# Cross network on one core: the first layer's weights in three loads, and a searched order begun 24 chunks sooner

## The chip, the cores and the metric

One core of a Trainium2 chip. TensorE multiplies into eight accumulator banks (PSUM); ScalarE (ACT in the profile) and VectorE (DVE) take results out; SyncE (SP) issues nearly all transfers; GpSimd (POOL) does little here. The metric is the device time of one execution in microseconds, the median of several; less is better.

## The reference

A cross network of six layers over 16384 rows of 416 features, in bf16:

```python
x = x0
for l in range(L):                                   # L = 6
    proj = jnp.einsum('bd,de->be', x, ws[l]) + bs[l]  # 416 x 416 weights
    x = x0 * proj + x
return x
```

## The kernel before, in words

**Tiles.** Data lies transposed: features on the 128 partitions, rows along the free axis. 416 features are three tiles of 128 and a tail of 32. The rows form eight groups of 2048, a group has four chunks of 512. A job (g, l) is layer l of group g. For each output tile i and chunk j it needs a product with three input tiles and with the tail: 13 quarters of 32 input rows. The tails of up to three jobs are made together, as a batch (`tails`, L700). ScalarE reads each finished bank and adds the bias (`tw`), VectorE multiplies by x0 and adds x (`x`). For tails the same is done into `ts` and `x3`.

**Recording.** `add` (L35) records each operation with what it reads and writes; `emit` (L149) writes the engines' queues and the semaphore waits out of that. Within an engine the order of recording is the order of execution, but for VectorE's sums, which can be held back by one place.

**The start.** `first_job` (L845) does job (0, 0). Group 0 is loaded in its natural layout by eight transfers (`load_nat`, L762; chunk j, halves of 2). TensorE turns it with an identity (`transposed_chunk`, L809), in two halves of six transposes each, and VectorE and ScalarE copy the results out of the banks (L828, L830). The first products (L673, by `full`) take the columns 0 to 256 of the first layer's weights, which one transfer brings (L772; the other columns come later, L777). `keep_busy` (L794) gives TensorE filler products. Then comes the first job's tail (L708, L720), and group 1.

**The written order.** After `first_job` the items (tiles and batches, in job order) up to the second output tile of job (0, 2) are written out whole tile by whole tile: `two_tiles` (L1141) for the first two tiles of job (1, 0), then the loop at L1160, which lets tail rows of two neighbouring tiles stand next to each other (`mode`). Products are full (L673), by columns of 32 (L667) or by rows of 32 (L694); four of the latter two kinds run beside each other.

**The searched run.** From there to the closing part, `stream` (L1085) splits every product into its 13 row quarters and places them on TensorE's four row strips independently. The order comes from a table: `ORDER` (L204) is a long text in which each letter names a strip and how old the chunk is that it turns to, and `|` stands for a batch of tails. `replay` (L231) walks through the table with fixed costs in units (20 to a product; `READ`, `NEXT`, `BACK` and so on for the reading engines), gives each product its place and each chunk its bank, and starts a chunk no sooner than a bank is free and its inputs from the layer before should be done (`needs`). Row products are L1129 (input tiles) and L1133 (tails); each finished chunk goes to `evacuate_chunk` (L562; L574 on ScalarE, L586 and L594 on VectorE). In a batch inside the run the second job's tail is read by VectorE alone (L636), the others by ScalarE (L640) and VectorE (L642); L644 is the tail sum.

**The end.** The last job of the last group is computed in natural layout (L1194), so that its results need no turning.

**Queues.** SyncE issues, in this order: two row loads, the first weights, six row loads, the tail weights of layer 0 (L401), the remaining columns, group 1's transposing loads (L411, L421), layers 1, 2 and 3, group 2, and so on.

Of the kernel before, what the change touches and what calls it, by code (L numbers as in the profile page):

```python
# [3 lines left out]
P = 128  # L4
CH = 512
# [16 lines left out]
class Program:  # L22
# [179 lines left out]
READ, NEXT, BACK, SECOND, PAIR, TAILS, SUMS = 19, 56, 70, 110, 56, 220, 240  # L202
LETTERS = "ABCDEFGHIJKLMNOPQRSTUVWXYZabcdefghijklmnopqrstuvwxyz0123456789"
ORDER = (  # L204
    "ABCDMBCTZOELBaAjZSIfFiQPVKHYBCcTVIDSJATKBQLWBQXKNALCZQLWBQCbMRLWBITWBQPCZMLWRALSBQLCRIbCRAPeJYWH"
    "N|AWPJQGDQBDWNITCJnQCZTIWBLQWNALWBQXCNIDWZIDWJYTCRbIWBLQBSbINWHAVCTUBOQLBaTARaDQZOLUSBDUORbICJbA"
    "aVTMGBPYBWPIRaHAORDYKBXQKBTIWBDUOZITCZIOTFADeRYPCNIbWQFPK|ABPWAVKPQBCPQVKDAVePQBKfMRaHJAbSIBKTAZ"
    "SLcNHCBQXBSMLBaAOXZQKHMVSDBQOXBMKXAVKDQVKDBMebUJOHAVObIRCLQBSfJ|EODBTAOZACbVcPKFAeXRYGPBYWPRAKPQ"
    "BiLMRGDNACbNAaXNISHBYCTNYCbVISPFAePBUKDVQaDRIOXFAOXBAObVQGLBcCXNAePZIWTFASPBcKPRUGDNAWDNQXCJAbWR"
    "APSJYDaRUDSJUfOF|ITCRIODJAbSJATJCQDOBPcWJDIeVbQOFXAVODUKBXQKBTIBaLQCZTAOQZLWFPAWNDUCNTUBOTIBaLQN"  # L210
    "WALVCQXBOQLBaTINWDIVODUCNXAOJXAWJDUeYBXOIZHSUBTOIBbCMZDWIZTO|EBPWQBOLAVCPQVKfMFSDARWPANXCUNSDIBS"
    "XYBTKAReLMVSbIBKTAhSLYNHCBQXNCMLWBAaPQVKDQBaPBUKjMZSXEBSPAZKPQVHCBQWDMRKXBIWDVAOXJAWfYJTCQZOLEBW"
    "DcRCTMJWbERKP|ABPWQBKPAVCPQVKDANebUBKXQNaHJASXIBKTAhSLYNHCBQXNCMLWBAaXQNKHAZWTMBKDYRKXNAWDNQXBOQ"
    "BObIRWDQBOTICfZAXaRIPFCYPBaUPCMVaLBIWDVQCPRICfJAebJUSPFAaPQVGL|MBDSNAPKBAObRUGLBAeXNYKHVAWTJAKTY"
    "BLCYRWDRIOXBIWPBUOLRAKbBAWPZQCLRYCbNIWTBISPBYKPRAeDQVPKAJXCURCPQJaDIBafQVGPBMaXRIOH|ABTOAZKPQBKD"
    "BUPaAVKbQdCbMRWLEBWTARKPYBWDNQKDZISXBIOTBAOfRYKDZQLWBQKXARKXMBWLBQCPZAWbJQGDQZWPBIWPQBOLAVCPQVKj"
    "MFSDARWPANXCUNSLEBSDYRCTIBafIVOTE|BPWRALOBcDOZQKXBIDVaITCRIbBSYLBSIXNaALVOQDKBQXKBITBaQLVOADOZXA"
    "WJAXSJYDSJYXOFQDZOAXBOQXBOQLBaITVCQDSZMLWBIXSBQLOBIbCZQLCZITWBQLBaITNWALVCUTBSATNaIDJWYTBSPAdOXY"
    "SF|AODVPAKNYXCBQXaJcHORAPaRIHCBUbCRMLWBIWTBQKPVALWRMGDBQCbRMWLBAWbNAKPZUCXQJaPBIWPBcKPVAWLMRCLBQ"
    "XCRMLWFAWTBQCPZAaPJAWbJMSDZcPCNXYSF|AOTBPAaBYSPJUGDdQODJMbWBIXOdAXKNQHCBQWDMRCbJAaTVIODJAfaUBXSc"  # L220
    "NKHAZSXIBLCVYLSNEXCMBWPIBWLAVCXQBOTAdaPUBOLQVaHJAbCMZSLUBSLARKfARWLMBKDYRCPRIbWBQXJOALBaQVCPISXB"
    "ASPYVKHMBCbNQeDJMSXZIP|FCATBaQPBOIDaVIDSJYDSZMXGJTASBjMCNULCVITBeQLNWADaRXMCJDYSBQPaJAbWRAjSJUPG"
    "dQLOBAPSBYPCVIPSBIDSVYDKRAbeJMXGBXMCVIPSBcLORALiNAXOJQDCNUTBOAXBeQPaBYLOVALWdMTGBYfSVMLG|ABWPAVK"
    "PQBCPVQCPJAebVAWLNQaHBYOXBUOLAVKbMRGDBQWDMRKXAJCbQVOLEBaXABOTYVGLMRWDIBSXIBTKAZSLMBKDQZKXARWDQNX"
    "KBISXNADOBcWbBMSXIZGDRYCTZIWPBIWfNQGLB|AWPRAKPBUCPRUKDJAbeJQPWFICXBUPChMLWFAWTBQKPVAWLNQCLBQCbMR"
    "WDJMWDVISPFAObBUCPVQKfNALWBQWLNACbRMLCYJTWARLW|AJTMWDJUCTVICTJWADVaMTBaNIDKVYTOBAfaNQLVGMTCJMSDA"
    "BXa"
# [3 lines left out]
def replay(tails, events, needs, keep):  # L231
# [15 lines left out]
    home, read, out, latest, due = {}, {}, [], [[]] * 4, list(events)  # L247
# [11 lines left out]
    for letter in ORDER:  # L259
        if letter == "|":  # L260
# [4 lines left out]
            on = at + 3 * SLOT * m + PHASE  # L265
            moved = [on + SLOT * k for k in parts]
# [40 lines left out]
def bass_standalone__cross_network_dcn__recsys_kernel(  # L307
# [82 lines left out]
    def load_wm(l, eng, f0=0, f1=D):  # L390
        toks = {0: [("wm", l)], W0: [("wm", l, "rest")]}[f0] if l == 0 else [("wm", l), ("wm", l, "rest")]
        add(eng, lambda h: h.dma_start(
            wm[l][:, :, f0:f1], ws[l, 0:NT * P, f0:f1].rearrange("(t p) f -> p t f", p=P)),
            writes=toks, lane=f"wm{l}_{f0}", batch=0)

    def wm_tok(l, i):
        return ("wm", l) if i < 2 else ("wm", l, "rest")
# [112 lines left out]
    def evacuate(g, l, i, banks, js, step, vector=()):  # L510
# [21 lines left out]
        while a <= js[-1]:  # L532
            if step > 1 and a % 2 == 0 and a + 1 <= js[-1] and banks[a + 1] == banks[a] + 1:
                w = 2
            else:
                w = 1
# [121 lines left out]
    def full(g, l, i, banks, first, chunk_major, after_chunk=None, chunks=range(NJ), ts_=range(NT), columns=False):  # L658
# [4 lines left out]
        for t, j in seq:  # L663
            if columns:
                for c in range(NJ):
# [5 lines left out]
                        reads=[stok(t, j), wm_tok(l, i)], writes=[("ps", banks[j])])  # L671
# [4 lines left out]
                reads=[stok(t, j), wm_tok(l, i)], writes=[("ps", banks[j])])  # L676
# [3 lines left out]
    def rows32(g, l, i, banks, first, small=False, inner=False):  # L680
        src, stok = x3_src(g, l)
        ecols = slice(i * P, (i + 1) * P)
        for j in range(NJ):
            r, q = quad(g, l, j)
            if small:
                for c in range(NJ):
                    o = slice(c * T32, (c + 1) * T32)
                    add("pe", lambda h, q=q, j=j, r=r, c=c, o=o: h.matmul(
                        psum[o, banks[j] * CH:(banks[j] + 1) * CH],
                        w3[l][q, i * P + c * T32:i * P + (c + 1) * T32], src[q, :],  # L690
                        start=first, stop=not first, tile_position=(r * T32, c * T32)),
                        reads=stok + [("w3", l, r)], writes=[("ps", banks[j])])
                continue
            add("pe", lambda h, q=q, j=j, r=r: h.matmul(  # L694
                bank(banks[j]), w3[l][q, ecols], src[q, :], start=first and not inner,
                stop=not first and not inner,
                tile_position=(r * T32, 0)),
                reads=stok + [("w3", l, r)], writes=[("ps", banks[j])])

    def tails(batch, corners_last=False, banks=None):  # L700
# [14 lines left out]
        for (g, l), b in zip(batch, bs_):  # L715
            src, stok = x_src(g, l)
            for t in range(NT):
                for j in range(NJ):
# [5 lines left out]
                        reads=[stok(t, j), wm_tok(l, NT)], writes=[("ps", b)])  # L724
# [47 lines left out]
    load_wm(0, "sp", 0, W0)  # L772
# [4 lines left out]
    load_wm(0, "sp", W0, D)  # L777
# [31 lines left out]
    def transposed_chunk(j):  # L809
# [3 lines left out]
        for k2 in (0, 2):  # L813
            for t in range(NT):
# [6 lines left out]
            if j == 0 and k2 == 0:  # L821
                keep_busy(2, 3)
        for t in range(NT):
# [20 lines left out]

    def first_job():  # L845
# [211 lines left out]
    mode = {}  # L1057
    prev = None
    for n, it in enumerate(items):
        if it[0] == "tails":  # L1060
            prev = None
        elif prev is None:
            mode[n] = "FR"
            prev = n
        else:
            mode[n] = "RF"
            prev = None
    for n in list(mode):
        if mode[n] == "FR" and not (n + 1 in mode and mode[n + 1] == "RF"):
            mode[n] = "F1"  # L1070

# [13 lines left out]
    def stream(run):  # L1085

        chunks, due = [], []
        for it in run:
            if it[0] == "tails":
                due.append(it[1])  # L1090
            elif it[1] not in order[-3:-1]:
                chunks += [(it[1], it[2], j) for j in range(NJ)]
# [8 lines left out]
        needs += [[]] * NJ  # L1101
        plan, read, left = replay([quad(g, l, j)[0] for (g, l), i, j in chunks] + [quad(LAST, L - 1, j)[0] for j in range(NJ)],
                                  [len(b) for b in due], needs, NJ)
        at = list(ring)
# [4 lines left out]
        for _, r, c, b in plan:  # L1109
# [14 lines left out]
            t = seen[c, r] = seen.get((c, r), -1) + 1  # L1124
            src, stok = x_src(g, l)
            s3, tok3 = x3_src(g, l)
            kw = dict(start=count[c] == 1, stop=count[c] == 4 * NT + 1, tile_position=(r * T32, 0))
            if t < NT:
                add("pe", lambda h, l=l, t=t, j=j, b=b, q=q, ecols=ecols, src=src, kw=kw: h.matmul(  # L1129
                    bank(b), wm[l][q, t, ecols], src(t, j, j + 1)[q, :], **kw),  # L1130
                    reads=[stok(t, j), wm_tok(l, i)], writes=[("ps", b)], row=r)
# [4 lines left out]
            if count[c] == 4 * NT + 1:  # L1136
# [4 lines left out]
    def two_tiles(g, l):  # L1141
# [17 lines left out]
    s_lo = items.index(("tile", (0, 2), 1))  # L1159
# [181 lines left out]
```

## Time and profile before

| | |
|---|---|
| median of 3 runs | 464.73 us (464.65 to 465.34) |
| the profiled execution | 464.88 us |
| its span, first to last instruction | 463.1 us |
| mean granted TensorE clock | 0.999 |
| instructions | 17845 |

The profile lists, by engine, how long it was busy; the timeline lists runs of like instructions by start, length, line, shape and count; a bracket behind a line gives the idle time before it and what ended it. Busy TensorE time overlaps within itself, because a product's end is modelled: the distance from start to start says more than a single length.

### The profile page before, as it was taken

To read this page: it belongs to the slowest core of one execution; us is meant where nothing else is said; L and a number is where in the kernel's file an instruction comes from. 1 tells how busy PE (TensorE), PEld (TensorE's weight loads), DVE (VectorE), ACT (ScalarE), POOL (GpSimd) and SP (SyncE) were. 2 spreads that over 40 slices of the span, in tenths; PEclk is the share of its full clock that TensorE was granted. 3 is DMA by queue.
4 is the path that set the end of the run, shared out by engine and by line. 5 is a ranking of instruction groups with operands and counts; after the bars stand their busy time and mean duration, and the time that the engine had idled before them with its cause. 6 is when DMAs were issued, how large, how long until landed. Compare 5 with 4: busy or idle time off the path is not lost.

```text
span 463.1 us, 17845 instructions
## 1 busy us (share of the span) xinstructions
PE 458.4 (99%) x8001; PEld 266.7 (58%) x8001; DVE 403.2 (87%) x697; ACT 381.9 (82%) x609; POOL 7.7 (2%) x16
## 2 busy tenths in 40 slices
PE   9999999999999999999999999999999999999996
PEld 5444656575655656565665556566556565555552
DVE  2897898988889898898989989898988988989997
ACT  4686889887988889798888979888888888888786
POOL 1000000000000000000000000000000000000010
PEclk9999999999999999999999999999999999999999
DMA  8986859000002859089656965590000079172799
GB/s 233 194 168 142 152 125 191 10 23 9 19 4 36 138 184 192 16 129 219 91 90 127 208 98 91 101 234 24 24 4 4 24 139 299 47 124 52 209 161 314
DMA packets 136128, 53.79 MB, mean 116 GB/s; under 512 B 113642, under 2 KB 134644, under 8 KB 136052
## 3 DMA queue, kind: packets, MB, share of 16 engines
q1 hardware_dynamic: 135896, 52.54, 54.3%
q8 instruction: 62, 1.02, 0.9%
q14 instruction: 14, 0.11, 0.1%
q10 hardware_dynamic: 156, 0.11, 0.1%
HBM read 5.97 MB, written 13.63 MB: 42 GB/s over the span
## 4 chain that ended last, share of the span: by engine, by line
PE 96%; DVE 2%; ACT 1%; issue 0%; DVEq 0%
PE ps L1129 74%; PE ps L720 7%; PE ps L1133 6%; PE ps L673 4%; PE ps L667 1%; PE ps L708 1%; DVE x L1255 1%; DVE x L1249 1%; PE ps L800 1%; PE ps L818 1%; ACT tw L574 1%; PE ps L694 1%; DVE tw L586 0%; DVE x L594 0%; DVE x L1217 0%
## 5 line engine op out<-in xcount | busy, mean ns | idle before, releaser
L1129 PE MATMUL ps<-x,wm 32*128 32x512 bf16 x6288 | 372.8, 374 | 0.0
L574 ACT ACTIVATE tw<-ps,bias 128x512 bf16<-128x512 f32 x524 | 326.9, 688 | 48.8 <-PE ps L1129 35.9
L1129 PEld LDWEIGHTS ps<-x,wm 32*128 32x128 bf16 x6288 | 222.3, 92 | 135.1 <-ACT tw L574 6.4
L586 DVE TENSOR_TENSOR tw<-tw,x 128x1024 bf16<-128x1024 bf16 x262 | 176.7, 688 | 41.1 <-ACT tw L574 39.5
L594 DVE TENSOR_TENSOR x<-tw,x 128x1024 bf16<-128x1024 bf16 x262 | 171.2, 688 | 0.3
L1133 PE MATMUL ps<-x,w 32*128 32x512 bf16 x524 | 159.5, 374 | 0.0
L1133 PEld LDWEIGHTS ps<-x,w 32*128 32x128 bf16 x524 | 44.6, 92 | 5.9
L720 PE MATMUL ps<-x,wm 128*32 128x512 bf16 x564 | 33.6, 380 | 0.0
L640 ACT ACTIVATE ts<-ps,bias 128x512 bf16<-128x512 f32 x32 | 20.4, 685 | 13.1 <-PE ps L708 13.1
L538 ACT ACTIVATE tw<-ps,bias 128x1024 bf16<-128x1024 f32 (+1 forms) x24 | 20.7, 938 | 8.2 <-PE ps L694 7.0
L720 PEld LDWEIGHTS ps<-x,wm 128*32 128x32 bf16 x564 | 13.5, 96 | 18.2 <-ACT tw L574 3.7
L673 PE MATMUL ps<-x,wm 128*128 128x512 bf16 x92 | 21.3, 380 | 0.0
L644 DVE TENSOR_TENSOR x<-ts,x 128x512 bf16<-128x512 bf16 x47 | 18.4, 419 | 0.3
L547 DVE TENSOR_TENSOR tw<-tw,x 128x1024 bf16<-128x1024 bf16 (+1 forms) x21 | 13.0, 636 | 2.2 <-ACT tw L538 2.1
L673 PEld LDWEIGHTS ps<-x,wm 128*128 128x128 bf16 x92 | 8.3, 98 | 11.4 <-issue 2.1
L636 DVE SCALAR_TENSOR_TENSOR ts<-ps,bias,x 128x512 bf16<-128x512 f32 x15 | 11.2, 746 | 3.1 <-PE ps L708 3.1
L552 DVE TENSOR_TENSOR x<-tw,x 128x1024 bf16<-128x1024 bf16 (+1 forms) x21 | 12.6, 634 | 0.0
L642 DVE TENSOR_TENSOR ts<-ts,x 128x512 bf16<-128x512 bf16 x32 | 12.4, 417 | 0.0
L956 POOL COPY ost<-ot 128x512 bf16<-128x512 bf16 x5 | 4.6, 922 | 367.3 <-DMA ot<-x 367.3
L1194 PE MATMUL ps<-wm,x 128*128 128x416 bf16 x48 | 9.3, 340 | 0.0
L828 DVE COPY x<-ps 128x512 bf16<-128x512 bf16 x5 | 2.0, 422 | 8.2 <-PE ps L818 8.1
L1243 ACT ACTIVATE x<-ps 128x416 bf16<-128x416 f32 x16 | 7.7, 529 | 1.5 <-PE ps L1194 1.5
(52 smaller groups left out, 74.1 us busy)
## 6 DMA issues: line engine op xcount, KB each, us to landing
out_dram<-ost SPq DMA_DIRECT2D x6, 1664.0 KB, 8.3
x<-x SPq DMA_DIRECT2D x24, 96.0 KB, 2.2
x<-in_x_dram SPq DMA_DIRECT2D x8, 208.0 KB, 4.2
x<-in_x_dram SPq DMA_DIRECT2D x4, 416.0 KB, 8.1
wm<-in_ws_dram SPq DMA_DIRECT2D x5, 312.0 KB, 3.5
x<-x SPq DMA_DIRECT2D x22, 64.0 KB, 2.5
out_dram<-x SPq DMA_DIRECT2D x3, 416.0 KB, 2.6
out_dram<-ost SPq DMA_DIRECT2D x2, 416.0 KB, 2.8
```

Source lines behind the costliest of these rows:

```text
L538: add("act", lambda h, a=a, w=w, b0=b0: h.activation(tw[r][:, a * CH:(a + w) * CH], psum[:, b0 * CH:(b0 + w) * CH], ACT_F.Identity, bias=b ...
L547: add("dve", lambda h, a=a, e=e: h.tensor_tensor(tw[r][:, a * CH:e * CH], tw[r][:, a * CH:e * CH], x0s[s0][:, i * GC + a * CH:i * GC + e * ...
L552: add("dve", lambda h, a=a, e=e: h.tensor_tensor(xs[so][:, i * GC + a * CH:i * GC + e * CH], tw[r][:, a * CH:e * CH], src(i, a, e), ALU.ad ...
L574: add("act", lambda h: h.activation(tw[r][:, j * CH:(j + 1) * CH], bank(b), ACT_F.Identity, bias=bias[:, i, l:l + 1], scale=1.0), reads=[( ...
L586: add("dve", lambda h: h.tensor_tensor(tw[r][:, o], tw[r][:, o], x0s[s0][:, c], ALU.mult), reads=[("tw", r, k) for k in both] + [x0_tok(s0 ...
L594: add("dve", lambda h: h.tensor_tensor(paired(xs[so][:, c], "p (k j q) -> p j k q"), paired(tw[r][:, o], "p (j k q) -> p j k q"), paired(s ...
L640: add("act", lambda h: h.activation(ts[r][:, :], bank(b), ACT_F.Identity, bias=bias[:, 3, l:l + 1], scale=1.0), reads=[("ps", b), "bias"], ...
L644: add("dve", lambda h: h.tensor_tensor(x3s[so][:, :], ts[r][:, :], res, ALU.add), reads=[("ts", r)] + rtok, writes=[("x3", so), ("x3", so, ...
L673: add("pe", lambda h, t=t, j=j: h.matmul(bank(banks[j]), wm[l][:, t, ecols], src(t, j, j + 1), start=(first and t == 0), stop=(not first a ...
L720: add("pe", lambda h, t=t, j=j, src=src, l=l, b=b, ro=ro, qo=qo: h.matmul(psum[qo, b * CH:(b + 1) * CH], wm[l][:, t, NT * P:D], src(t, j, ...
L1129: add("pe", lambda h, l=l, t=t, j=j, b=b, q=q, ecols=ecols, src=src, kw=kw: h.matmul(bank(b), wm[l][q, t, ecols], src(t, j, j + 1)[q, :], ...
L1133: add("pe", lambda h, l=l, b=b, q=q, ecols=ecols, s3=s3, kw=kw: h.matmul(bank(b), w3[l][q, ecols], s3[q, :], **kw), reads=tok3 + [("w3", l ...
```

## The change

Four things are done together.

1. The first layer's first 256 columns come as three transfers of one input tile each, in the order 1, 0, 2, in place of one.
2. In the first layer's first two chunks, the products go by input tile, both output tiles for each, in the order in which the copies come (`by_copy`, `by_input_tile`); the transposes use the same order; the second half of chunk 2's transposes stands behind chunk 1's products; one filler is 2 and not 5 units of 128 columns.
3. `two_tiles` does the whole first tile of job (1, 0) alone and of the second tile only the products of input tile 0 for chunks 0 and 1; its results are read bank by bank. The loop in written order and `mode` are gone: all other items go to `stream`, which so has 24 more chunks. The first two chunks have one input tile less to do there.
4. `ORDER` is a new table. `replay` knows about the begun chunks (`ahead`), and about when a layer's tail is to be expected after its batch (`TURN`, `SHIFT`); the inputs of the first 36 chunks are expected six products later (`LATE`). The starting times of the banks and of ScalarE are new, and jobs (0, 1) and (0, 2) go by halves of two chunks.

```diff
 FENCE, PHASE, CHANGE = 22, 52, 9
-READ, NEXT, BACK, SECOND, PAIR, TAILS, SUMS = 19, 56, 70, 110, 56, 220, 240
+READ, NEXT, BACK, SECOND, PAIR, TAILS, SUMS, SHIFT = 19, 56, 70, 110, 56, 220, 240, 215
+TURN, LATE = (200, 150, 260), 6
...
-    size = [[3 + (r == tails[c]) if c < n - keep else 2 * (r == tails[c]) for r in range(4)] for c in range(n)]
-    free, flight, begun, act = [0] * 4, {}, 0, 156
-    banks = [(0, 0), (0, 1), (0, 2), (0, 3), (84, 4), (84, 5), (178, 6), (178, 7)]
+    size = [[3 - (c < ahead) + (r == tails[c]) if c < n - keep else 2 * (r == tails[c]) for r in range(4)] for c in range(n)]
+    free, flight, begun, act = [0] * 4, {}, 0, 243
+    banks = [(0, 0), (0, 1), (0, 2), (0, 3), (89, 4), (145, 5), (201, 6), (257, 7)]
...
+        if r == tails[c] and after[c][0] >= 0:
+            start = max(start, ons[after[c][0]] + after[c][1] - 3 * SLOT * (c < n - keep))
...
+    def load_wm_tile(t):
+        add("sp", lambda h: h.dma_start(wm[0][:, t, 0:W0], ws[0, t * P:(t + 1) * P, 0:W0]),
+            writes=[("wm", 0, t)], lane=f"wm0_{t}", batch=0)
...
-    load_wm(0, "sp", 0, W0)
+    for t in (1, 0, 2):
+        load_wm_tile(t)
...
+    def by_copy(j):
+        return (0, 2, 1) if j == 1 else (1, 0, 2)
+
+    def by_input_tile(j, *bks):
+        src, stok = x_src(0, 0)
+        for n, t in enumerate(by_copy(j)):
+            for i, b in enumerate(bks):
+                add("pe", lambda h, n=n, t=t, i=i, b=b: h.matmul(
+                    bank(b[j]), wm[0][:, t, i * P:(i + 1) * P], src(t, j, j + 1),
+                    start=n == 0, stop=False), reads=[stok(t, j), ("wm", 0, t)], writes=[("ps", b[j])])
...
-        keep_busy(5, 3)
+        keep_busy(2, 3)
...
-        full(g, l, 0, ba, True, True, chunks=[0])
-        full(g, l, 1, bb, True, True, chunks=[0])
+        by_input_tile(0, ba, bb)
         transposed_chunk(1)
-        transposed_chunk(2)
-        full(g, l, 0, ba, True, True, chunks=[1])
-        full(g, l, 1, bb, True, True, chunks=[1])
+        transposed_chunk(2, (0,))
+        by_input_tile(1, ba, bb)
+        transposed_chunk(2, (2,))
         transposed_chunk(3)
...
-                chunks += [(it[1], it[2], j) for j in range(NJ)]
+                if it[1] not in order[1:4:2]:
+                    chunks += [(it[1], it[2], j) for j in range(NJ)]
+                elif not it[2]:
+                    chunks += [(it[1], i, j) for a in (0, 2) for i in range(NT) for j in (a, a + 1)]
...
-            needs.append([(t, *p) for t, p in enumerate(pairs) if c - max(p) < 30])
+            needs.append([(t - LATE * (c < 3 * 3 * NJ), *p) for t, p in enumerate(pairs) if c - max(p) < 30])
...
-        for i in (0, 1):
-            full(g, l, i, bks[i], True, False, ts_=[0], columns=True)
+        for i, chunks in ((0, range(NJ)), (1, range(2))):
+            full(g, l, i, bks[i], True, False, chunks=chunks, ts_=[0], columns=True)
         full(g, l, 0, bks[0], True, False, ts_=[1, 2], columns=True)
         rows32(g, l, 0, bks[0], False)
-        evacuate(g, l, 0, bks[0], list(range(NJ)), 2)
-        finish_tile(g, l)
-        rows32(g, l, 1, bks[1], False, inner=True)
-        full(g, l, 1, bks[1], False, False, ts_=[1, 2])
-        evacuate(g, l, 1, bks[1], list(range(NJ)), 2)
+        evacuate(g, l, 0, bks[0], list(range(NJ)), 2, single=True)
         finish_tile(g, l)
...
-    s_lo = items.index(("tile", (0, 2), 1))
-    for n, it in enumerate(items[:s_lo]):
...
-    bka, left = stream(items[s_lo:])
+    _, (g, l), i = items[0]
+    start_job(g, l)
+    two_tiles(g, l)
+    bka, left = stream(items[1:])
```

More of the change, by code (lines that the diff above doesn't have):

```diff
@@ L388, in bass_standalone__cross_network_dcn__recsys_kernel, with load_wm, wm_tok @@
     W0 = 2 * P
-    def load_wm(l, eng, f0=0, f1=D):
-        toks = {0: [("wm", l)], W0: [("wm", l, "rest")]}[f0] if l == 0 else [("wm", l), ("wm", l, "rest")]
+    def load_wm(l, eng, f0=0):
+        toks = [("wm", l, "rest")] if f0 else [("wm", l, t) for t in range(NT)]
         add(eng, lambda h: h.dma_start(
[L393 to L397, printed above, removed]
+            wm[l][:, :, f0:D], ws[l, 0:NT * P, f0:D].rearrange("(t p) f -> p t f", p=P)),
+            writes=toks, lane=f"wm{l}", batch=0)
+    def load_wm_tile(t):
+        add("sp", lambda h: h.dma_start(wm[0][:, t, 0:W0], ws[0, t * P:(t + 1) * P, 0:W0]),
+            writes=[("wm", 0, t)], lane=f"wm0_{t}", batch=0)
+    def wm_tok(l, i, t):
+        return ("wm", 0, "rest") if l == 0 and i > 1 else ("wm", l, t)
     def load_w3(l, eng):
@@ L532, in evacuate @@
         while a <= js[-1]:
-            if step > 1 and a % 2 == 0 and a + 1 <= js[-1] and banks[a + 1] == banks[a] + 1:
+            if not single and step > 1 and a % 2 == 0 and a + 1 <= js[-1] and banks[a + 1] == banks[a] + 1:
                 w = 2
@@ L675, in full, with rows32 @@
                 start=(first and t == 0), stop=(not first and t == NT - 1)),
-                reads=[stok(t, j), wm_tok(l, i)], writes=[("ps", banks[j])])
+                reads=[stok(t, j), wm_tok(l, i, t)], writes=[("ps", banks[j])])
             if after_chunk and t == NT - 1:
                 after_chunk(j)
-    def rows32(g, l, i, banks, first, small=False, inner=False):
+    def rows32(g, l, i, banks, first):
         src, stok = x3_src(g, l)
@@ L684, in rows32 @@
             r, q = quad(g, l, j)
[L685 to L693, printed above, removed]
             add("pe", lambda h, q=q, j=j, r=r: h.matmul(
-                bank(banks[j]), w3[l][q, ecols], src[q, :], start=first and not inner,
-                stop=not first and not inner,
+                bank(banks[j]), w3[l][q, ecols], src[q, :], start=first, stop=not first,
                 tile_position=(r * T32, 0)),
@@ L812, in transposed_chunk @@
         place = ((ba, 0), (bb, 0), (ba, CH)) if j == 0 else ((ba, 0), (ba, CH), (bb, 0))
-        for k2 in (0, 2):
-            for t in range(NT):
+        for k2 in halves:
+            for t in by_copy(j):
                 b, o = place[t]
@@ L822, in transposed_chunk @@
                 keep_busy(2, 3)
+        if 2 not in halves:
+            return
         for t in range(NT):
@@ L1123, in stream @@
             q, ecols = slice(r * T32, (r + 1) * T32), slice(i * P, (i + 1) * P)
-            t = seen[c, r] = seen.get((c, r), -1) + 1
+            begun = c < 2
+            t = seen[c, r] = seen.get((c, r), 0 if begun else -1) + 1
             src, stok = x_src(g, l)
             s3, tok3 = x3_src(g, l)
-            kw = dict(start=count[c] == 1, stop=count[c] == 4 * NT + 1, tile_position=(r * T32, 0))
+            whole = 4 * (NT - begun) + 1
+            kw = dict(start=count[c] == 1 and not begun, stop=count[c] == whole, tile_position=(r * T32, 0))
             if t < NT:
@@ L1130, in stream @@
                     bank(b), wm[l][q, t, ecols], src(t, j, j + 1)[q, :], **kw),
-                    reads=[stok(t, j), wm_tok(l, i)], writes=[("ps", b)], row=r)
+                    reads=[stok(t, j), wm_tok(l, i, t)], writes=[("ps", b)], row=r)
             else:
```

108 lines of the change are left out of this document (40 added, 68 removed).

## The prediction

> **What bounds the kernel now.** I read the page's busy table first, then the chain of waits, then TensorE's timeline up to 45 us, then the copies' engines over the same stretch.
>
> ```profile
> span 463.1 us, 17845 instructions
> PE 458.4 (99%) x8001; PEld 266.7 (58%) x8001; DVE 403.2 (87%) x697; ACT 381.9 (82%) x609; POOL 7.7 (2%) x16
> ...
> PE 96%; DVE 2%; ACT 1%; issue 0%; DVEq 0%
> ```
>
> TensorE is busy 99% of the span and holds 96% of the chain that ended last. So only two things can shorten the run: fewer or denser TensorE instructions, or less waiting inside what shows as busy. The timeline (start, length, line, shape, count) shows where it is not dense:
>
> ```profile
> 5.78 1.53 PE L673 MATMUL ps<-x,wm 128*128 128x512 bf16 x6
> 7.14 1.55 PE L818 MATMUL ps<-ident,x 128*128 128x128 bf16 x24
> 8.54 1.46 PE L673 MATMUL ps<-x,wm 128*128 128x512 bf16 x6
> ...
> 12.36 0.40 PE L694 MATMUL ps<-x,w 32*128 32x512 bf16 x4
> ...
> 14.64 2.76 PE L673 MATMUL ps<-x,wm 128*128 128x512 bf16 x12
> ...
> 18.31 3.62 PE L667 MATMUL ps<-x,wm 128*32 128x512 bf16 x64
> 21.87 0.61 PE L694 MATMUL ps<-x,w 32*128 32x512 bf16 x8
> ...
> 40.48 0.83 PE L1129 MATMUL ps<-x,wm 32*128 32x512 bf16 x12
> ```
>
> Twelve full products take 2.76 us, the last 0.38: (2.76 - 0.38) / 11 = 0.216 us from start to start. I call that a slot; four 32-row or 32-column products share one (64 at 18.31 take 16 slots, 3.46 us; the next line starts at 21.87, so the change of shape costs 0.10). The searched run begins at 40.48 and the closing part (L1194) at 447.77.
>
> **The change, part 1: 24 chunks move into the searched run.** Before, TensorE goes from 18.31 to 40.48 = 22.17 us by written order: 112 L667 (28 slots), 24 L694 (6), 56 L673 (56), 16 L688 (1), 24 L720 (6): 97 slots, 20.95 us, and 8 small L708. So 1.22 us is overhead: the joints between kinds, and those 8. After, the instruction order has 56 of the 32-column kind (14 slots), 4 L694 (1), and 304 more row products in the run (7124 against 6820: 76 slots) with one more batch of tails, two jobs (24 products, 6 slots): the same 97 slots, in fewer kinds.
>
> What the run costs per slot, from its own trace: 447.77 - 40.48 = 407.29 us for 6820 / 4 + 44 x 3 = 1837 slots, 396.8 us, and 15 batches of tails. A batch (L720 at 57.96, run resumed at 60.37, 9 slots between) costs 2.41 - 1.94 = 0.47 beyond its slots; 15 make 7.05. What is left, 3.45 us or 0.85%, are its empty places. So the moved stretch costs 14 x 0.216 + 0.10 + 0.22 (L694) + 82 x 0.216 + 0.47 + 0.85% of 18.2 (0.15) = 21.67 us: **0.50 less** than 22.17. The 0.85% is the old order's; the new order is another one over all 552 chunks, and each tenth of a per cent of it is 0.43 us either way. I keep 0.85% and hold that as a bound.
>
> **Part 2: what is late next.** The run now starts at about 21.7 instead of 40.5, while VectorE still works off the first layer. It is nearly without idle time from 14.2 to 32.3; ScalarE alone frees the accumulators, so VectorE's lag reaches TensorE only through next-layer inputs. Those of group 0, layer 1 end at 22.78 (its last L552) and 23.57 (its tail, L644). In the new order the first product that reads that layer comes 4 to 5 slots after the run's start, at 22.7, and reads first the tile that has been done since 17; the tail is read after 25.8. No wait. The first that can bite is the tail of layer 2 of group 0. In the new order its first reader stands 14 products of its row behind the first batch, 14 x 0.216 = 3.03 us after the run resumes. Behind that product stand all four rows, and the accumulators they would free. What the tail takes on VectorE is counted from these rows:
>
> ```profile
> 192.64 0.75 DVE L636 SCALAR_TENSOR_TENSOR ts<-ps,bias,x 128x512 bf16<-128x512 f32 x1 [0.33 <-PE ps L708]
> 193.31 0.68 DVE L594 TENSOR_TENSOR x<-tw,x 128x1024 bf16<-128x1024 bf16 x1
> 193.91 0.69 DVE L586 TENSOR_TENSOR tw<-tw,x 128x1024 bf16<-128x1024 bf16 x1
> 194.51 0.42 DVE L644 TENSOR_TENSOR x<-ts,x 128x512 bf16<-128x512 bf16 x1
> ...
> 31.95 0.75 DVE L644 TENSOR_TENSOR x<-ts,x 128x512 bf16<-128x512 bf16 x2
> ```
>
> The resume there was at 192.49. In the new order VectorE has, from the batch on: one L636 (0.67 to the next start), a product of 1024 (0.60), a tail sum (0.34), a sum of 1024 (0.60), a tail product (0.34), the tail sum (0.42). Begun 0.15 after the resume, it ends at 3.12, and TensorE starts 0.06 later: 3.18 against 3.03, a **wait of 0.15**. The bounds: the first job's tail ended between 1.9 and 4.2 us after the resume in the searched run's batches (no wait, to 1.2), and 4.95 in the written stretch (31.95 + 0.42 against a resume at 27.41), where VectorE was behind: 1.98.
>
> **Part 3: the first layer.** Removed: 3 x 128 columns of filler at 5.30. Moved: the transposes of tile 1 go first, so VectorE's copy starts two transposes (2 x 0.107) sooner, at 4.70, and ends at 5.13; the new order starts on that tile. The weights now come by tile, 64 KB each; the single load landed at 5.51, the first third sooner. TensorE then starts at 5.43, not 5.78, and no longer waits at 6.0 and 6.3 for ScalarE's two copies (done 5.73 and 6.22): six products end at 6.73, not 7.14. That is 0.41 won, but it is given back:
>
> ```profile
> 8.02 1.70 ACT L830 ACTIVATE x<-ps 128x512 bf16<-128x512 bf16 x3 [1.72 <-PE ps L818]
> 10.59 1.09 ACT L830 ACTIVATE x<-ps 128x512 bf16<-128x512 bf16 x2 [0.88 <-PE ps L818]
> ```
>
> Only 18 of 24 transposes (0.056 each) now stand ahead of chunk 1's products, which then wait for VectorE's copy (0.26 after the last transpose, 0.42 long): they start at 8.08 and end at 9.38. Chunk 2's last six transposes come only then, so its two ScalarE copies move from 8.6 to 9.80, and chunk 3's two stand behind them in ScalarE's queue: 9.80 + 3 x 0.494 + 0.595 = 11.88, against 11.68 now. TensorE reaches the last copy's reader at 11.69, waits until 11.93, and L694 starts at 12.45, against 12.36: **0.09 lost**. [...]
>
> The loads: two more issues on SyncE put everything behind them (six row loads, L401, the rest of the weights, group 1's transposes, layers 1 to 3) 0.93 us later in its queue (0.465 each). The six row loads land 0.5 to 0.8 apart between 6.1 and 9.45, though issued 0.48 apart, each 4 to 4.9 us after its issue: the engines are full there (DMA share 1.06 from 5 to 10 us), so I take 0.1 to 0.2 us of delay, inside the slack of TensorE's reads. Group 1's last transpose landed at 19.30 and is read at 20.6, layer 1's weights at 20.73 and are read at 22.7: 0.93 later still holds. [...]
>
> **The sum**: -0.50 + 0.15 + 0.09 = -0.26. The profiled execution took 464.88 us (span 463.1, 1.78 around it); 464.62. The median shown is 464.73, 0.15 below that execution: **464.5 us**. About 0.2% (0.93 us) is what a measurement of this kernel can tell from no change, so this is no change.
>
> **The rivals.**
> - Denser (0.18): chunk 3's copies are not late, the tail does not wait, and the new order has a tenth of a per cent fewer empty places: -0.50 - 0.41 - 0.43 = -1.34, 463.4. For it: TensorE has no other work and the order decides all. Against: ScalarE's queue, counted above.
> - Slower (0.14): VectorE is still behind at the first batch, as it was at 27.41. Place: the first reader of layer 2's tail of group 0. Price: 1.98, less the 0.15 I counted, gives +1.57, 466.3. The wait is as long as VectorE starts that batch after the resume: from 0.41 on the gain is gone, from 1.34 on the loss passes 0.2%. Against: ahead of the batch the new order has 18 sums and products of 1024 behind the tail that ends at 23.57; 18 x 0.60 puts their end at 34.4, and the run resumes 66 slots after its start, at 36.0.
> - The loads are late (0.14): issue, not bandwidth, sets the landings, all 0.93 later. Then chunk 2's first transposes wait for a row load at 8.4, and what follows moves by 0.68: +0.42, 465.15. For it: the first load's first part lands 1.96 us after its issue, so the third load, issued at 3.04, could not begin to land before 5.0, where it now begins at 4.59. Against: from the fifth load on, the present landings are later than issue plus 1.96 even so. [...]
> - The forecast itself: 0.54.
>
> Faster by over 0.2%: 0.18; slower: 0.14; within: 0.54 + 0.14 = 0.68. The range must reach both near rivals: 463.4 to 465.5, leaving out the slower case (0.14).
>
> **What would show it.** The first products (L854) at 5.4 and chunk 1's transposes at 6.7; L694 at 12.4 to 12.5; the run's first row product at 21.6 to 21.8; its length to the closing part 425.6. Wrong: a TensorE wait on a DMA before 12 us; a gap of over 0.3 us some 3 us after the first batch's resume; a run over 0.5 us off 425.6.

## The result, and the profile after

The changed kernel takes **466.71 us** (466.35 to 467.19, 5 runs) against 465.00 (464.65 to 465.59) for the kernel before on the same chip: ratio 1.0035, 95% interval 1.0025 to 1.0046. It is slower by 1.7 us where I forecast no change, and lies outside my range.

The page of the changed kernel; the q8 line is of its part on transfer queues (packets, MB, share of 16 engines):

```profile
span 464.9 us, 18166 instructions
...
PE 457.9 (98%) x8156; PEld 264.6 (57%) x8156; DVE 404.9 (87%) x697; ACT 384.5 (83%) x619; POOL 6.7 (1%) x16
...
q8 instruction: 64, 1.05, 0.9%
...
PE 90%; DVE 4%; SPq 3%; DMA 1%; issue 1%; DVEq 0%
```

In the chain that ended last, TensorE falls from 96% to 90%; SyncE's queue (SPq) and transfers appear with 4%. Before, the q8 line had 62 packets; my prediction made no use of it.

TensorE's timeline of the changed kernel shows where the chain leaves TensorE:

```profile
5.03 1.46 PE L854 MATMUL ps<-x,wm 128*128 128x512 bf16 x6
6.80 1.05 PE L818 MATMUL ps<-ident,x 128*128 128x128 bf16 x12 [0.31 <-DMA x<-in_x_dram]
8.17 0.51 PE L818 MATMUL ps<-ident,x 128*128 128x128 bf16 x6 [0.32 <-DMA x<-in_x_dram]
8.52 1.46 PE L854 MATMUL ps<-x,wm 128*128 128x512 bf16 x6
...
12.89 0.39 PE L694 MATMUL ps<-x,w 32*128 32x512 bf16 x4
...
18.84 2.33 PE L676 MATMUL ps<-x,wm 128*32 128x512 bf16 x40
21.48 1.05 PE L676 MATMUL ps<-x,wm 128*32 128x512 bf16 x16 [0.31 <-DMA x<-in_x_dram]
22.46 0.40 PE L694 MATMUL ps<-x,w 32*128 32x512 bf16 x4
22.68 0.60 PE L1135 MATMUL ps<-x,wm 32*128 32x512 bf16 x8
```

Three brackets name a load as what TensorE waited for. The 40 products at 18.84 are 10 slots, 2.16 us; the next would start at 21.00 and start at 21.48, a wait of 0.48.

Stage by stage, from the two timelines, one profiled execution each (span of before 463.1, of after 464.9):

| stage | before | after | difference |
|---|---|---|---|
| start to the first L694 | 12.36 | 12.89 | +0.53 |
| from there to group 1's first product | 5.95 | 5.95 | 0 |
| from there to the closing part | 429.46 | 429.26 | -0.20: +0.48 for the wait, -0.68 for the rest |
| closing part to the start of its last twelve products | 9.16 | 9.48 | +0.32 |
| from there to the end of the span | 6.17 | 7.32 | +1.15 |
| sum | 463.1 | 464.9 | +1.80 |

So the move itself won 0.68. The largest loss is behind TensorE's last products, and the next in the loads.

**What is late at the end.** The transfer view of both kernels from 455 to 465 us, in slices of 0.25 us (what was moved):

```profile
GB/s 413 333 359 413 333 359 399 346 406 353 373 359 406 433 399 399 399 386 413 413 426 306 286 406 187 97 300 320 137 0 0 0 0 0 0 0 0 0 0 0
```

```profile
GB/s 359 393 413 413 306 413 340 346 432 353 359 353 339 353 366 393 420 413 426 379 400 413 413 413 213 399 366 73 223 283 336 50 27 20 23 10 0 0 0 0
...
q8 instruction: 1, 0.02, 0.7%
```

Before (the first line), the stores fill the engines (busy 90% or more in all but one slice up to 460, at 333 to 433 GB/s) and all end near 462.2. After, all but a trickle is done by 462.75; then five slices move 10 to 50 GB/s, about one engine's share (the stores move some 380 until then, and 380 / 16 = 24). The window holds one q8 packet. By the trace's transfer records it starts at 457.05, is 16 KB and takes 1.1 us. The landings fit: of the 16 parts of the next store, 15 land from 459.32 to 459.52 and one at 461.25, and each later store has one such part, down to 464.42 for the last.

**My theory** was now: queue q8 carries TensorE's instructions, one packet to 256 of them (in both traces the nth packet starts between 91 instructions ahead of 256 n and 87 behind). Before, the trace has 16025 TensorE instructions (a product counts two, with its weight load) and the 62nd packet is the last (447.32); after, 16338, and the 64th comes among the last stores. **The rivals**: every added instruction costs some time; or the end is late because of the new order or the loads.

### The profile page after: what moved, and what is told of

Read it like the earlier page. It is cut to its first block, busy times and chain, and to the rows that moved or that the text cites. A ratio compares the mean times of both kernels' runs of the same rounds, so it can differ in the third digit from the quotient of the medians.

```text
span 464.9 us, 18166 instructions
## 1 busy us (share of the span) xinstructions
PE 457.9 (98%) x8156; PEld 264.6 (57%) x8156; DVE 404.9 (87%) x697; ACT 384.5 (83%) x619; POOL 6.7 (1%) x16
## 4 chain that ended last, share of the span: by engine, by line
PE 90%; DVE 4%; SPq 3%; DMA 1%; issue 1%; DVEq 0%
PE ps L1135 75%; PE ps L719 7%; PE ps L1139 6%; PE ps L707 1%; SPq L420 1%; DMA x<-in_x_dram 1%; DVE tw L595 1%; DVE x L1231 1%; DVE x L1237 1%; DVE x L603 1%; SPq L762 1%; SPq L430 1%; SPq L402 0%; SPq L410 0%; PE ps L676 0%
## 5 line engine op out<-in xcount | busy, mean ns | idle before, releaser
L1135 PE MATMUL ps<-x,wm 32*128 32x512 bf16 x6568 | 389.2, 374 | 0.0
L583 ACT ACTIVATE tw<-ps,bias 128x512 bf16<-128x512 f32 x548 | 342.6, 687 | 49.1 <-PE ps L1135 34.4
L1135 PEld LDWEIGHTS ps<-x,wm 32*128 32x128 bf16 x6568 | 227.7, 92 | 143.9 <-ACT tw L583 4.9
L595 DVE TENSOR_TENSOR tw<-tw,x 128x1024 bf16<-128x1024 bf16 x274 | 184.8, 688 | 39.1 <-ACT tw L583 37.5
L603 DVE TENSOR_TENSOR x<-tw,x 128x1024 bf16<-128x1024 bf16 x274 | 180.3, 691 | 0.8
L1139 PE MATMUL ps<-x,w 32*128 32x512 bf16 x548 | 165.0, 374 | 0.0
L547 ACT ACTIVATE tw<-ps,bias 128x512 bf16<-128x512 f32 (+1 forms) x11 | 8.0, 808 | 4.5 <-PE ps L694 4.5
L832 ACT ACTIVATE x<-ps 128x512 bf16<-128x512 bf16 x7 | 3.7, 600 | 5.6 <-PE ps L818 5.6
L707 PE MATMUL ps<-x,w 32*32 32x512 bf16 x188 | 7.1, 385 | 0.0
L1176 PEld LDWEIGHTS ps<-wm,x 128*128 128x128 bf16 x48 | 4.2, 98 | 4.8 <-issue 1.5
```

The costliest lines, as they stand in the source:

```text
L583: add("act", lambda h: h.activation(tw[r][:, j * CH:(j + 1) * CH], bank(b), ACT_F.Identity, bias=bias[:, i, l:l + 1], scale=1.0), reads=[( ...
L595: add("dve", lambda h: h.tensor_tensor(tw[r][:, o], tw[r][:, o], x0s[s0][:, c], ALU.mult), reads=[("tw", r, k) for k in both] + [x0_tok(s0 ...
L603: add("dve", lambda h: h.tensor_tensor(paired(xs[so][:, c], "p (k j q) -> p j k q"), paired(tw[r][:, o], "p (j k q) -> p j k q"), paired(s ...
L707: add("pe", lambda h, l=l, b=b, s3=s3, ri=ri, qi=qi, ro=ro, qo=qo: h.matmul(psum[qo, b * CH:(b + 1) * CH], w3[l][qi, NT * P:D], s3[qi, :], ...
L1139: add("pe", lambda h, l=l, b=b, q=q, ecols=ecols, s3=s3, kw=kw: h.matmul(bank(b), w3[l][q, ecols], s3[q, :], **kw), reads=tok3 + [("w3", l ...
L1176: add("pe", lambda h, t=t: h.matmul(bank(b, n=D), xcol(t, j, kk), wm[l][:, t, :], start=(first and t == 0), stop=(not first and t == NT - 1)),
```

## The experiments

Each ratio is against the kernel before, timed beside it on the same chip (464.94 for runs 1 to 4; 465.05 for 5 to 8; 465.02 for 9 to 11; 465.30 for 12). The time is a median of 5 or 11; the trace is of one execution, which can lie off it: of run 2 it is the fastest (464.98), of 4, 8 and 9 the slowest (465.63, 466.46, 468.44).

**1. One load of weights** in the changed kernel (a_one_load): `for t in (1, 0, 2): load_wm_tile(t)` becomes the single transfer of before.

> The changed kernel with the first weights in one transfer again, the products still by input tile. Theory 1 (SyncE's queue): two issues fewer put the row loads and group 1's transposing loads about 1 us sooner; the row-load waits before 10 us and the wait for group 1's last tile (0.48 us) go, the run starts about 0.9 us sooner (21.8 instead of 22.7), and the whole is 0.8 to 1.1 us below the changed kernel: some 465.7, still 0.7 above the kernel before, since the slow end stays. Theory 2 (the loss is VectorE's lag behind the earlier run and at the close): the loads do not matter, within 0.2 us of 466.7.

466.70, ratio 1.0036 (1.0022 to 1.0049): no gain. Its TensorE timeline:

```profile
5.91 1.88 PE L855 MATMUL ps<-x,wm 128*128 128x512 bf16 x6 [0.20 <-DMA wm<-in_ws_dram]
...
8.97 1.58 PE L855 MATMUL ps<-x,wm 128*128 128x512 bf16 x6 [0.18 <-DVE x L831]
...
13.47 0.39 PE L694 MATMUL ps<-x,w 32*128 32x512 bf16 x4
```

The row loads and group 1 are no longer late, as expected, but the first products wait for the weights, chunk 1's for VectorE's copy, and L694 comes at 13.47. So the run starts at 22.77, not sooner, and my expectation failed: with one load the order by input tile starts no earlier than the old one (5.91; 5.78 before), and only six of chunk 2's transposes, not twelve, cover VectorE's copy.

**2. 84 instructions fewer** (a_full_products): group 1's 56 column products become 14 full ones, which take the same 14 slots.

```diff
-            full(g, l, i, bks[i], True, False, chunks=chunks, ts_=[0], columns=True)
-        full(g, l, 0, bks[0], True, False, ts_=[1, 2], columns=True)
+            full(g, l, i, bks[i], True, False, chunks=chunks, ts_=[0])
+        full(g, l, 0, bks[0], True, False, ts_=[1, 2])
```

> The changed kernel with the 56 products by columns of 32 as 14 full ones: the same sums, 42 products fewer. Theory 1 (in the closing part a 16 KB packet of TensorE's instructions is fetched at 457.05 and holds one transfer engine for 1.1 us, so the last stores land late): 84 instructions fewer, and the 64th packet is not needed any more; from the start of the last twelve products to the end of the span 6.2 us instead of 7.3, the whole 1.0 to 1.2 us below the changed kernel, about 465.6. Theory 2 (the last stores are late because VectorE and the last batch are late): no change at the end, within 0.2 us of 466.7.

465.47, ratio 1.0009 (1.0001 to 1.0018): 1.2 us better than the changed kernel, as expected. 63 packets, the last at 448.27; from the start of the last twelve products to the end it takes 6.15 us.

**3. 92 instructions more in the kernel before** (b_more_instr): fillers of 128 columns (`m = 1`) and eight products of group 1 by columns.

> The kernel before with 46 more products of no more work: the fillers singly, 8 full products of group 1 by columns of 32. Theory 1: 92 more instructions reach the next packet (the 63rd) within the last microseconds, and the last stores land late as in the changed kernel: 1.0 to 1.3 us above the kernel before, all of it behind the last twelve products. Theory 2: 0 to 0.2 us above it.

466.43, ratio 1.0033 (1.0021 to 1.0046). The last twelve products start at 456.79, sooner than before (456.93), yet the span ends 7.6 us behind them, at 464.4. The 63rd packet started at 454.69. Nothing of the change is in this kernel, and it has the loss at the end.

**4. Edits 1 and 2 together** (a_one_load_full).

> Both edits together, one transfer of weights and full products. Theory 1: both losses go, 1.9 to 2.2 us below the changed kernel, about 464.6 and so 0.3 to 0.5 below the kernel before. Theory 2: within 0.3 us of the changed kernel.

465.16, ratio 1.0005 (0.9996 to 1.0013), 1.55 below the changed kernel where I expected 1.9 to 2.2: the end is mended (6.2), the start is not (L694 at 13.38).

**5. The move alone, with full products** (a_old_first_full): the new run behind the first layer of before (one load, old order, fillers of 5), and edit 2.

> The moved run alone: the changed kernel with the first layer, its one load and its products in the old order, and with full products in group 1's start, so that no packet of instructions is fetched in the last microseconds. Theory 1 (the first layer's new order and its loads cost about 0.5 us at L694 and 0.3 to 0.5 at group 1's last tile; the move itself wins 0.5 to 0.7; the close loses 0.3): L694 at 12.4, run from 21.8, 0.2 to 0.5 us below the kernel before, about 464.6. Rival (the moved run is itself what costs, because VectorE is behind): 0.3 or more above the kernel before.

**464.52**, ratio 0.9991 (0.9983 to 1.0000), L694 at 11.97, the run from 21.40. The fastest of all; the interval just reaches no change.

**6. Chunk 2's transposes whole** (a_whole_chunk2_full): `transposed_chunk(2)` ahead of chunk 1's products, not in two parts, and edit 2.

> The changed kernel with full products in group 1's start and all twelve transposes of chunk 2 ahead of chunk 1's products; three loads and products by input tile stay. If what delays L694 is that chunk 2's copies on ScalarE start late (and its first product has to wait for both, as it writes the bank that they empty), L694 comes 0.3 to 0.5 us sooner than with the halves apart (12.3 to 12.5 against 12.77), and the whole is 0.2 to 0.5 us below 465.47, unless group 1's last transposing load then holds TensorE. If the late row loads set it, it is the same as before to 0.1 us, or later, since the second half waits for its load ahead of the products.

465.69, ratio 1.0013 (1.0005 to 1.0022). TensorE now waits 0.69 for a row load until 8.47, and L694 comes at 13.30: it is the second case, the late row loads set it.

**7. Two of the weight loads from ScalarE's queue** (a_act_loads_full): `load_wm_tile(t, "act")` for tiles 0 and 2, and edit 2.

> The changed kernel with full products and two of the three weight loads issued by ScalarE in place of SyncE. If SyncE's two added issues are what delays the row loads and group 1, the row loads land as in the kernel before (the last at 9.4, not 10.3), group 1's last tile at 19.3 to 20 and not 21.4, and the whole is 0.1 to 0.5 us below 465.47. If the queue does not matter, no difference; ScalarE's first copy is at 5.1 and should not be held.

465.83, ratio 1.0017 (1.0008 to 1.0026): no gain in time. But SyncE's queue is as it was before, and the row loads land as before: the last at 9.33 (9.45 before, 10.28 in the changed kernel), and group 1's last at 20.36. The weights pay for it. ScalarE issues its two at 1.33 and 1.73, beside SyncE's at 1.65; tile 1's, which is needed first, lands at 5.68 (4.49 in the changed kernel), TensorE waits for it until 5.82, and chunk 1's products start at 8.79.

**8. Only the three loads, in the kernel before** (b_three_loads): the transfer split by tile, nothing else.

> The kernel before with only the load split in three. SyncE's queue: all that follows is issued 0.9 to 1.4 us later; the row loads land 0.6 to 0.8 later and TensorE waits some 0.5 for them, and again for group 1's last tile (read at 20.9): 0.5 to 1.0 us above the kernel before. If the engines' bandwidth and not the issue sets the landings: within 0.2 us of it.

465.85, ratio 1.0017 (1.0008 to 1.0026), 0.80 slower. Its timeline:

```profile
8.44 0.51 PE L823 MATMUL ps<-ident,x 128*128 128x128 bf16 x6 [0.47 <-DMA x<-in_x_dram]
9.20 0.51 PE L823 MATMUL ps<-ident,x 128*128 128x128 bf16 x6 [0.24 <-DMA x<-in_x_dram]
...
13.37 0.40 PE L697 MATMUL ps<-x,w 32*128 32x512 bf16 x4
...
22.30 1.05 PE L670 MATMUL ps<-x,wm 128*32 128x512 bf16 x16 [0.22 <-DMA x<-in_x_dram]
```

Two waits on row loads, L694 (here L697) a microsecond late, and the wait at group 1: the split alone makes them. (The trace is of the slowest execution; the price is the median's 0.80.)

**9. 110 instructions more in the changed kernel** (a_more_instr): fillers of 128 columns, and the first job's third tile by columns.

> The changed kernel with 55 more TensorE products and the same arithmetic: the fillers go 128 columns at a time (19 more), and the third output tile of job (0, 0) goes by columns of 32 (48 for 12). TensorE has 110 more instructions (16448 for 16338), all of them in the first 16 us, where the filler's work is the same and 48 column products take the 12 slots of the 12 full ones. If the cost at the end is the place of the 64th instruction packet, it now comes 110 instructions sooner, near 451 us in place of 457.05, and is over before the last stores: 6.2 us from the start of the last twelve products to the end in place of 7.32, and 465.5 to 465.7 in all, in spite of more instructions. If every added instruction costs time (the two earlier runs could be read so: 84 fewer were faster, 92 more were slower), 467.0 or more. If the end is late for another reason, 466.7 to 466.9.

467.48, ratio 1.0047 (1.0034 to 1.0061). **A miss**, and by its number the rival's. Two places of the trace explain the slowest execution, which it shows (468.44). At the start, TensorE waits for group 1's last load far longer:

```profile
23.12 1.05 PE L676 MATMUL ps<-x,wm 128*32 128x512 bf16 x16 [1.85 <-DMA x<-in_x_dram]
```

The products were due at 21.10. The third packet starts at 21.07; 15 of the load's 16 parts land from 21.39 to 21.59, and one at 23.08. At the end (454 to 459 us, slices of 0.125):

```profile
GB/s 359 386 346 346 451 240 266 271 161 162 164 187 152 79 52 31 59 37 13 27 27 27 27 12 18 18 207 289 289 393 383 373 413 399 413 399 413 426 426 426
...
q8 instruction: 1, 0.02, 1.2%
```

The packet starts at 454.53, when a store (issued at 452.71) and the last transposing transfer (issued at 453.70) are under way. Of the store's parts 3 land at 455.3 to 455.4 and 13 at 457.3 to 457.5, the transposing transfer lands at 458.3, and for 1.6 us at most 79 GB/s are moved. From then on the stores fill the engines to the end, so the delay is never made up: 7.4 behind the last twelve. "Over before the last stores", as I had put it, was not early enough. That more instructions cost time wherever they stand, this run does not rule out; run 12 does.

**10. ScalarE for the last batch** (a_last_batch_act), on the kernel of 5: `vector=k == 1 and (LAST, L - 2) not in batch`.

> The fastest kernel so far (new run, old first layer, full products in job (1, 0): 464.52) with one edit: in the last batch of tails the second job's tail is read by ScalarE and multiplied by VectorE (0.34 to the next start), where VectorE alone read it (0.67). If VectorE's lag is what makes the closing part 0.3 longer (it has no gap from this batch to the closing part's transposes, and the ninth L1178 product starts when its sum ends), the closing part from its first product to the start of the last twelve takes 9.2 in place of 9.48, and the kernel 464.2 to 464.3. If ScalarE's extra 0.6 comes back as a late bank, or the wait in the closing part has another cause, it stays at 464.5 or goes to 464.7.

465.24, ratio 1.0005 (0.9996 to 1.0014). The closing part takes 9.25, not 9.48, but from the last batch's resume to it TensorE needs 8.52, not 7.92: ScalarE's 0.6 came back in full, as the rival said, and the kernel is slower by more than either case (464.7 at most). Two kernels without the edit have 9.27 and 9.28 as well (1 and 11), so it doesn't prove the cause of the 0.32 either.

**11. The move alone, with column products** (a_old_first): kernel 5 without edit 2, 16338 instructions.

> The searched run of the changed kernel with the whole first layer as before (one load of weights, old order), and job (1, 0)'s products by columns of 32 as in the changed kernel: the move alone. TensorE has 16336 instructions, two fewer than the changed kernel, so if the 64th packet decides, it falls into the last stores as there, and the gain of the move is lost: 465.5 to 465.8, with 7.2 to 7.4 us behind the start of the last twelve products. If the packet's place is not what decides, 464.5 to 464.7, as with full products.

465.94, ratio 1.0014 (1.0003 to 1.0024), a little above what I expected; packet at 456.47, 7.6 behind the last twelve. The run's gain can be read here without a wait: 447.20 - 18.43 = 428.77 from group 1's first product to the closing part, against 429.46: **-0.69**. The packet takes it and more.

**12. The packet moved alone** (a_split_tails): 192 instructions more, none ahead of 58 us. In batches 2 to 5 the tail products of input tiles 1 and 2 go in two halves:

```diff
+                    parts = 2 if t and batch_n[0] in (2, 3, 4, 5) else 1
+                    w = CH // parts
+                    for u in range(parts):
...
+                            psum[qo, b * CH + u * w:b * CH + (u + 1) * w], wm[l][:, t, NT * P:D],
+                            src(t, j, j + 1)[:, u * w:(u + 1) * w],
```

> The changed kernel with its tail products of input tiles 1 and 2 in the second to fifth batch (58 to 150 us) issued as two of 256 columns instead of one of 512: the same columns and arithmetic, 96 more products, 192 more TensorE instructions (16530 for 16338), none of them before 58 us, so that the instruction packets among the first loads stay as in the changed kernel. The 64th packet should move from 457.05 back to about 446, where in the kernel before, too, one fell and cost nothing; the 65th would need about 80 instructions more. If a packet costs only from about 450 us on, where the stores fill the transfer engines to the end (in the run with 110 more instructions it fell at 454.5, stopped a transposing store for 1.9 us and the end was just as late), then from the last twelve products to the end it takes 6.1 to 6.3 in place of 7.32, and the kernel 465.4 to 465.8, up to 0.2 more if the split costs at the joints. If more instructions cost time wherever they stand, 467.2 or more; if the end of the changed kernel is late for another reason, 466.6 to 467.0, with 7.3 behind the last twelve.

**465.41**, ratio 1.0007 (0.9998 to 1.0016): 1.3 us better than the changed kernel with 192 more instructions. From its page and its timeline:

```profile
q8 instruction: 64, 1.05, 1.0%
```

```profile
457.46 2.28 PE L1183 MATMUL ps<-wm,x 128*128 128x416 bf16 x12
```

As many packets as after, but the last at 447.12, and 463.6 - 457.46 = 6.1 behind the last twelve. The split batch takes 2.07 (60 products from 58.32 to 60.39) against 2.06 (36), so the instructions themselves cost nothing here. This settles it for the end: the place of the last packet decides.

All 14 kernels, one execution each, by the start of the last packet:

| last packet | kernels | last twelve to the end |
|---|---|---|
| 447.0 to 449.2 | before, 2, 4, 5, 6, 7, 8, 10, 12 | 6.1 to 6.4 |
| 454.5 to 457.4 | after, 1, 3, 9, 11 | 7.3 to 7.6 |

## Why the prediction was wrong, point by point

- **Part 1, the move: right, the size a little low.** Predicted -0.50 and a run of 425.6; measured -0.68 and 425.42, with part 2's wait in the measured ones. Counted as there (1919 slots, 16 batches), the new order has 3.40 us or 0.80% of empty places, not 0.85%.
- **Part 2, the tail's wait: right.** Predicted ready 3.18 after the resume and read 0.15 late; measured 3.25 (resume 36.96, VectorE's sum ends 40.21, its reader starts 40.26), after 59 products that take 3.19: 0.11 late. The rival of a VectorE that lags falls. Its price of 1.98 was misread: 27.41 is where that batch starts, and TensorE resumes behind it at 28.72, so the same sum gives 0.68.
- **Part 3, the loads: wrong.** The steps that failed: "each 4 to 4.9 us after its issue: the engines are full there ... so I take 0.1 to 0.2 us of delay", and "0.93 later still holds". The last row load landed 0.83 later (10.28 for 9.45) and group 1's last 2.13 later (21.43 for 19.30), where I had left slack for 1.3. All traces say the same: with three loads in SyncE's queue (after, 2, 6, 8, 9, 12) the last row load lands at 9.78 to 10.49 and group 1's last at 20.64 to 23.08; with one (the other eight, run 7 among them) at 9.22 to 9.72 and 19.30 to 20.62. So the queue sets when the row loads land, and the rival "the loads are late" was the right mechanism; b_three_loads alone lost 0.80, where I had priced the lateness at 0.68 (+0.42 with the rest). The two added issues cost what I had counted; SyncE's lines in before, after and a_full_products (2):

```profile
1.65 0.43 SPq L392 DMA_DIRECT2D wm<-in_ws_dram  x1
```

```profile
1.65 1.81 SPq L402 DMA_DIRECT2D wm<-in_ws_dram  x3
```

```profile
1.66 1.38 SPq L402 DMA_DIRECT2D wm<-in_ws_dram  x3
```

  In 2 the row loads behind them are issued 0.96 later than before, in after 1.38. The 0.42 between is the first weight issue, 0.86 long instead of 0.43; it is as long (0.79 to 0.84) in four kernels with a single load (3, 4, 5, 11), so the split does not make it. The three loads land at 4.49, 4.70 and 5.00, sooner than the one of before (5.51): what moved was SyncE's queue.
- **Part 3, the first layer: right but for the loads.** 0.09 predicted at L694, 0.53 measured. The 0.44 between is there before chunk 1's products start (8.52, not 8.08): chunk 2's first transposes wait for their row load until 8.17. From there on the forecast holds: 4.37 to L694 predicted and measured, and ScalarE's four copies take 2.06, where I had counted 2.08:

```profile
10.23 2.06 ACT L832 ACTIVATE x<-ps 128x512 bf16<-128x512 bf16 x4 [1.87 <-PE ps L818]
```

  I overlooked that chunk 2's first product writes the bank into which chunk 2 was transposed, so that it waits for two of these copies (the second ends at 11.32, the product starts at 11.38). It cost nothing: the last product waits for the last copy either way (12.30, 12.36). By loads and order, L694 comes at 11.97 to 12.48 (old order, one load: before, 3, 5, 10, 11), 13.37 (old order, three), 13.38 and 13.47 (new, one), 12.77 to 13.22 (new, three: after, 2, 9, 12). Each edit needs the other, and together they still lose to the old start.
- **The closing part and the end: not in the sum.** I took all behind the run as unchanged: the sum has no term for it, and no reason is given. This is the step that cost most: +0.32 and +1.15. The 313 instructions that I counted only as slots carry the 64th packet into the last stores; runs 3 and 12 show it. The +0.32 is read from the trace, and its cause is not proved: TensorE resumes behind the last batch 7.92 ahead of the closing part, before it was 9.61; VectorE's pair of sums (L603) ends at 450.70, and the ninth product of the second group waits for it. The first line is before, where that group's ten products start without a gap; the rest is after:

```profile
448.71 1.92 PE L1194 MATMUL ps<-wm,x 128*128 128x416 bf16 x10
```

```profile
448.10 0.88 PE L1176 MATMUL ps<-wm,x 128*128 128x416 bf16 x4
...
449.04 1.57 PE L1176 MATMUL ps<-wm,x 128*128 128x416 bf16 x8
450.76 0.53 PE L1176 MATMUL ps<-wm,x 128*128 128x416 bf16 x2
```

```profile
449.01 1.69 DVE L603 TENSOR_TENSOR x<-tw,x 128x1024 bf16<-128x1024 bf16 x2
```

By medians against each one's own before: the move -0.53 (5; the 0.32 of the closing part is in it), the new first layer +1.06 (2 less 5), the packet +1.18 (after less 2): +1.71. Other pairs give the packet +1.54 (1 less 4) and +1.45 (11 less 5). My -0.26 had the sign of the first of these; the other two were not in it. Of the three signs that I had named for a wrong forecast one appeared, TensorE's waits on transfers before 12 us; the gap behind the first batch and a run off 425.6 did not.

What stays open: why VectorE's pair of sums takes 1.28 in some executions, 1.49 or 1.69 in others; why SyncE's first weight issue takes 0.43 or 0.8; and how much of group 1's wait belongs to packets and how much to the queue. In the four kernels with the new start (2, 12, after, 9) the last load landed at 20.64, 21.24, 21.43 and 23.08, and TensorE waited 0, 0, 0.48 and 1.85; of the 1.85, 1.49 is the one late part, from 21.59 to 23.08.

## What to carry to other kernels

Count an edit's instructions as well as its slots: see where the last instruction packet falls, and if it falls among the closing stores (which cost 1.2 to 1.5 us here), take instructions out (or put some in early) to move it. A load cut in three costs its queue two issues more (0.95 us here), and the loads behind them land later (0.3 to 1.0 at the last row load), even where the transfer engines look full (share 1.06 from 5 to 10 us in the kernel before). And take no stage as unchanged because the edit doesn't touch it: here the end had transfers that a packet could meet, and products that wait for VectorE.

## What the runs showed of the hardware

- The packets of q8 follow TensorE's instruction count: the nth starts some 30 instructions ahead of 256 n (from 91 ahead to 87 behind in the kernels before and after). A packet is 16 KB and takes 0.9 to 1.6 us in these two. TensorE was not seen to wait for one: the new run takes 425.4 to 425.5 in 1, 2, 4, 5, 6, 9, 11, 12 and after, wherever they fall (426.0 in 10, by its edit, and 425.8 in 7, where TensorE loses 0.4 once, near 343 us, while ScalarE waits for VectorE). The transfers that it met did wait. Transposing loads nearly stopped from some 0.3 us behind its start to 0.8 behind its end; here the changed kernel's from 13 to 17 us, in slices of 0.1, with a packet from 13.88 to 14.82:

```profile
GB/s 92 128 184 246 243 269 269 289 445 269 259 131 44 3 0 0 0 0 10 8 8 8 10 10 10 13 246 287 289 294 289 287 287 260 292 297 287 287 289 294
```

  From 14.2 to 15.6 at most 44 GB/s. Where only plain stores were under way (after, at 457.05), they went on, but one part of 16 of each landed 1.2 to 1.7 later than the others. In mid-run TensorE waits for none of that; at the end 1.2 to 1.5 us were lost where a packet came at 454.5 or later, and some 1.5 where one met a load that TensorE was about to read (9).
- The same first transposes go at 0.107 or at 0.056 us each in different executions. The trace's record of a full granted clock begins 3.56 to 6.79 us into the span (5.16 before, 4.16 after), and ahead of it there is none. Where it begins among these transposes (3, 5, 10 and after), the pace changes from 0.107 to 0.056 there. With the old start it begins at 3.65, 3.56, 4.20, 5.16 and 6.16, and L694 comes at 11.97, 12.10, 12.25, 12.36 and 12.48 (5, 3, 10, before, 11): the first layer can't be judged to less than 0.5 from one execution.
